# Gate and value as seven block products of 256 columns in place of two accumulations of 512, in an attention and gated feed-forward kernel

## The chip, the cores and the metric

The kernel runs on one core of a Trainium2 chip. The metric is the device time of one execution in microseconds (us). The kernel before took 1326.7 us, the median of three runs (1326.5 to 1326.91).

## The reference

```python
def phi(x):                                   # q is 8 x 8 x 576 x 64, w_phi 64 x 128
    proj = np.einsum('bhsd,df->bhsf', x, w_phi)
    proj = proj - np.max(np.abs(proj), axis=-1, keepdims=True)
    return np.concatenate([np.exp(proj), np.exp(-proj)], axis=-1)
q_p, k_p = (phi(q), phi(k))
kv = np.einsum('bhsf,bhsd->bhfd', k_p, v)
num = np.einsum('bhsf,bhfd->bhsd', q_p, kv)
den = np.einsum('bhsf,bhf->bhs', q_p, np.sum(k_p, axis=2))[..., None] + 1e-06
x = (num / den), heads side by side: 4608 tokens x 512
rms = np.sqrt(np.mean(x * x, axis=-1, keepdims=True) + 1e-06)
xn = x / rms * rms_g
g = xn @ w_gate                               # 512 x 1536
silu = g * (1.0 / (1.0 + np.exp(-g)))
val = xn @ w_val                              # 512 x 1536
out = silu * val @ w_out                      # 1536 x 512
```

## The kernel before

Every matrix is kept as a high part and a remainder in the type fp32r (`_split`: the high part by ScalarE, L60, and the remainder, the "low", by VectorE (DVE) or GpSimd (POOL), L61). A product is three matmuls: high weight by high x, high weight by low x, low weight by high x.

The work goes in three stages. The attention stage writes x transposed to DRAM (`xs`) and decodes the feed-forward weights, which arrive as 8-byte numbers (`_decode`, L48 to L55: two ScalarE passes, DVE passes L50, L51, L52, two GpSimd products L54, a DVE addition L55). Within it and just behind it, gate and value of the first `J1` = 3 column tiles are computed from x not yet normalised ("fills", L461) and stored as `gvs`.

The gate/value stage is the place of the change. It takes the tokens in nine blocks of `T` = 512 and the remaining `JN` = 9 column tiles of 128. For each block and tile `gv` (L641) accumulates gate and value in one PSUM bank each, in 2 x 12 matmuls of 128x512. The banks come from a pool of six, `gp`; two further banks, `fp`, serve the row sums. `hidden` applies silu to the gate bank on ScalarE (L626), multiplies by the value bank on DVE (L628) and stores h to DRAM. `gv_raw` (L652) brings the three tiles of the fills into the same path: it multiplies them by the reciprocal norm `ri` on DVE, then `hidden`.

While a block's tiles run, `prep(bk + 1)` prepares the next block in seven pieces, placed behind tiles 0, 2, 3, 4, 5, 6 and 7: load x; squares on ScalarE added up on GpSimd (L571, L572); a sum over partitions by two matmuls with ones (L580, L581) and a square root on ScalarE (L583); reciprocals (L587) and the normalised x (L592) on DVE; the split of x into `xb` with its lows on GpSimd. The pieces of `decs` decode w_out, 24 of them, one behind every second tile; `load_o` forms the sums of w_out that the output stage uses (L671). A Tile framework adds the waits; each engine executes its instructions in the order in which the code issues them.

```python
for n, j in enumerate(order):
    gv(bk, j)
    if n % 3 == 1:
        gv_raw(bk, n // 3, r.pop(n // 3))
    ...
    if n in pieces:
        pieces[n]()
    if (bk, n) in slots:
        slots[bk, n]()
```

The output stage (matmul line L802) multiplies h by w_out in 18 groups of 256 tokens. It uses seven products of block sums already, 126 matmuls of 128x256 a group.

## Time and profile before

| | |
|---|---|
| median of three runs | 1326.7 us |
| the profiled execution, its time and its span | 1327.53 us, 1325.0 us |
| TensorE (PE) busy, whole span | 1286.6 us (97%) |
| DVE, ScalarE (ACT), GpSimd (POOL) busy | 901.7, 689.9 and 645.3 us |
| mean granted TensorE clock | 0.993 |
| attention stage, with most fills | 0 to 505 us |
| last fills | 505 to 592 us |
| gate/value stage | 592 to 1049 us |
| output stage | 1049 to 1322 us |

In the lines of the profile, a group is "line engine operation, output<-inputs, shape and type, count | busy us, mean ns of one | idle time of the engine just before it and what ended it". A line of the timeline begins with the start and the duration in us; matmul durations there overlap, so the pace is read from the starts. A line of windows gives the window, its length, the busy time of each engine with the number of instructions, the granted clock in parts of full speed, the share of the DMA engines' time and GB/s. PEld is TensorE's loading of weights, which runs beside its matmuls.

### The profile page before, as it was taken

Reading aid. Unit: us, or ns where it says so; the run is one execution under the profiler, and the core shown is the slowest. Engines: PE = TensorE matmul, PEld = TensorE weight load, DVE = VectorE, ACT = ScalarE, POOL = GpSimd, SP = SyncE. Lnnn points to the kernel's source line nnn. Section 1 sums busy time; section 2 is a strip of 40 time slices with the busy share of each in tenths; the row PEclk is TensorE's granted clock in tenths of the full one; section 3 lists DMA queues with packets and bytes.
Section 4 is the critical chain, followed back from the end, with each engine's and each line's share of the span. In section 5 each row is a group of like instructions: output and inputs, shape, how many; then the busy total and the mean of one; then the engine's idle time right before and its main releaser. Section 6 shows DMA issues by size and latency. Waiting matters only on the chain. (4 is left out here: it accounts for less than half of the span.)

```text
span 1325.0 us, 23881 instructions
## 1 busy us (share of the span) xinstructions
PE 1286.6 (97%) x8742; PEld 1188.3 (90%) x8742; DVE 901.7 (68%) x1232; ACT 689.9 (52%) x1455; POOL 645.3 (49%) x580
## 2 busy tenths in 40 slices
PE   7989999999999989999999999999999999999998
PEld 7989999999999989998888877888888799999998
DVE  7898888788878763214366663665344389989994
ACT  5987877788777774453244333333232243433431
POOL 3765655556555563631141322421310178888884
PEclk9999999999999999999999999999999999999999
DMA  5556666665556529633343535544326134543441
GB/s 157 130 143 159 162 175 173 181 179 160 158 174 171 151 64 267 225 127 98 132 164 127 182 115 176 176 139 147 127 95 206 57 112 128 168 151 128 156 163 48
DMA packets 195299, 197.10 MB, mean 149 GB/s; under 512 B 68784, under 2 KB 151856, under 8 KB 195184
## 3 DMA queue, kind: packets, MB, share of 16 engines
q1 hardware_dynamic: 195184, 195.60, 48.6%
q8 instruction: 69, 1.13, 0.4%
q14 instruction: 46, 0.38, 0.1%
HBM read 126.04 MB, written 69.50 MB: 148 GB/s over the span
## 5 line engine op out<-in xcount | busy, mean ns | idle before, releaser
L641 PE MATMUL gp<-xb,w 128*128 128x512 f32 x1296 | 302.5, 393 | 1.7 <-DVE h L628 1.7
L641 PEld LDWEIGHTS gp<-xb,w 128*128 128x128 f32 x1296 | 243.4, 188 | 58.0 <-DVE h L628 3.0
L367 POOL TENSOR_TENSOR ql<-eq,qh 128x256 fp32r<-128x256 f32 x256 | 217.2, 879 | 76.2 <-issue 52.6
L61 POOL TENSOR_TENSOR xo<-st,xo 128x768 fp32r<-128x768 f32 x54 | 124.2, 2312 | 112.2 <-ACT xo L60 112.2
L54 POOL TENSOR_TENSOR wa<-raw,wa 128x192 f32<-128x192 f32 (+1 forms) x112 | 64.9, 600 | 165.8 <-DVE wa L52 120.0
L302 DVE TENSOR_REDUCE mx<-pp 128x4 f32<-128x512 f32 (+1 forms) x160 | 101.1, 633 | 47.7 <-PE pp L300 46.0
L338 PE MATMUL acc<-vm,ek 128*128 128x65 f32 x1024 | 131.4, 268 | 0.6 <-ACT ek L325 0.5
L338 PEld LDWEIGHTS acc<-vm,ek 128*128 128x128 f32 x1024 | 127.3, 192 | 1.2 <-ACT ek L325 1.2
L60 ACT CAST xo<-st 128x768 fp32r<-128x768 f32 x54 | 43.4, 835 | 152.0 <-DVE st L755 75.0
L626 ACT ACTIVATE sl<-gp 128x512 f32<-128x512 f32 x81 | 48.0, 594 | 135.4 <-PE gp L641 115.3
L61 POOL TENSOR_TENSOR xb<-x,xb 128x1024 fp32r<-128x1024 f32 x18 | 50.7, 2834 | 139.1 <-ACT xb L60 139.1
L628 DVE TENSOR_TENSOR h<-sl,gp 128x512 f32<-128x512 f32 x81 | 55.2, 683 | 87.9 <-PE gp L641 56.6
L363 ACT ACTIVATE qh<-sm 128x512 fp32r<-128x512 f32 (+1 forms) x192 | 97.2, 506 | 0.0
L461 PE MATMUL fp<-xo,fg 128*128 128x288 f32 x576 | 93.2, 301 | 2.7 <-ACT fo L464 2.2
L298 PE MATMUL pp<-wh,th 128*128 128x256 f32 x288 | 87.8, 306 | 2.7 <-DVE yr L305 2.1
L362 ACT ACTIVATE eq<-sm 128x512 f32<-128x512 f32 x128 | 78.4, 613 | 18.2 <-PE sm L351 17.4
L652 DVE TENSOR_TENSOR gvr<-gvr,ri 128x1024 f32<-128x1024 f32 x27 | 33.1, 1228 | 78.1 <-DMA gvr<-gvs 77.9
L461 PEld LDWEIGHTS fp<-xo,fg 128*128 128x128 f32 x576 | 81.1, 190 | 4.1 <-ACT fo L464 3.3
L300 PE MATMUL pp<-wh,tl 128*128 128x256 f32 x288 | 83.1, 297 | 1.3 <-DVE tl L61 1.3
L802 PE MATMUL gy<-wh,xo 128*128 128x256 f32 x432 | 80.1, 283 | 2.4 <-ACT xo L60 1.4
L299 PE MATMUL pp<-wl,th 128*128 128x256 f32 x288 | 81.7, 285 | 0.0
L641 PE MATMUL gp<-xb,fv 128*128 128x512 f32 x324 | 79.8, 395 | 1.0 <-DVE h L628 1.0
(167 smaller groups left out, 3428.5 us busy)
## 6 DMA issues: line engine op xcount, KB each, us to landing
hs<-h SPq DMA_DIRECT2D x108, 256.0 KB
gvs<-fo SPq DMA_DIRECT2D x96, 144.0 KB
gvr<-gvs SPq DMA_DIRECT2D x27, 512.0 KB
fg<-hs SPq DMA_DIRECT2D x9, 1536.0 KB
fv<-hs SPq DMA_DIRECT2D x9, 1536.0 KB
rc<-di SPq DMA_DIRECT2D x32, 288.0 KB
x<-xs SPq DMA_DIRECT2D x16, 576.0 KB
x<-xs SPq DMA_DIRECT2D x9, 1024.0 KB
```

The source lines that it names most:

```text
L61: (lo_eng or nc.vector).tensor_tensor(lo, x, hi.bitcast(F32), ALU.subtract)
L298: nc.tensor.matmul(o, th[:, cs], wh, start=True, stop=False)
L299: nc.tensor.matmul(o, th[:, cs], wl, start=False, stop=False)
L300: nc.tensor.matmul(o, tl[:, cs], wh, start=False, stop=True)
L302: nc.vector.tensor_reduce(mx[:, 0:2 * m], pp[:, 0:2 * m], axis=AX.X, op=ALU.max, apply_absolute_value=True)
L338: nc.tensor.matmul(acc[:, sg, h], e[h][:, sg, j], vm[:, h, j], start=False, stop=(h == 1 and j == T0 - 1))
L362: nc.scalar.activation(ei[:, sg], yi, AF.Exp, scale=1.0 - 2.0 * sg)
L363: nc.scalar.activation(hi[:, sg], yi, AF.Exp, scale=1.0 - 2.0 * sg)
L367: nc.gpsimd.tensor_tensor(lo[:, sg, cs], ei[:, sg, cs], hi[:, sg, cs].bitcast(F32), ALU.subtract)
L461: nc.tensor.matmul(fp[:, 0:TF], w, xx[x][:, c], start=(i == 0), stop=(i == 3 * NC - 1))
L641: nc.tensor.matmul(o, w, e[:, c], start=(i == 0), stop=(i == 3 * NC - 1))
L802: nc.tensor.matmul(place[n], a[:, kp], w[:, o], start=(first and kp == 0 and i == 0), stop=(kp == KP - 1 and i == 2), skip_group_check=True)
```

## The change

The two 512-wide accumulations become one 2 x 2 block product by the Strassen-Winograd scheme: the rows of the left matrix are gate and value, those of the right one the halves `LO` and `HI` (256 tokens each) of the block, and the inner dimension is halved too. A unit (block and tile) is then seven products p1 to p7, each 6 matmuls of 128x256 over 256 of the 512 inner values.

- *Accumulators.* Three banks, `A`, `B` and `E`, with two buffers each, in place of the six `gp`. p1 and then p2 go to A (the gate of LO). ScalarE copies p1's sum from A into B, where p6 is added; ScalarE copies that to SBUF as `u2`, then p7 is added; DVE adds B to `c22` (ScalarE's copy of p5 from E), then p4 is added to B: the value of LO. p3 is added to E, and DVE adds E to u2: the gate of HI. c22 is the value of HI. silu follows on ScalarE, the product for LO on DVE (L719), that for HI on GpSimd (L723).
- *Order.* `product` fixes the order on TensorE with `issue_after`; the old unit's p7, p3 and p4 stand between products of the new one: p1, p5, p7 of the old, p2, p6, p3 and p4 of the old.
- *Operands.* `prep` makes seven splits 512 wide for each block (four block sums on DVE, lows on GpSimd) in place of two 1024 wide, and `prep_w` the seven sums of the weights once, for six tiles during the last fills and for three in block 0.
- *Elsewhere.* `gv_raw` goes in halves of 256 tokens: product with `ri` on DVE (L737), silu on ScalarE, product on GpSimd (L739). The jobs are placed by a table `jobs` at four points of a unit. All of w_out's sums are formed in the last block, into slots of gate/value weights that are done with; decodes run in blocks 1 to 6, four each. The fills use two `fp` and two `A` banks in place of two `fp` and six `gp`; `raws` has two buffers in place of three; the h of the output stage goes to three slots in place of two.

```diff
-    ps_g = pool(pg_ctx, "m_ps_g", 6, space=PSUM)
-    gp = lambda: ps_g.tile([128, 512], F32, name="gp")
+    ps_g = pool(pg_ctx, "m_ps_g", 2, space=PSUM)
+    bank = lambda n: ps_g.tile([128, 512], F32, name=n)
...
+    def product(o, n, x, w, first):
+        last = next(i for i in reversed(nc.cur_bb.bb.instructions) if i.engine == mybir.EngineType.PE)
+        with tc.issue_after(last):
+            product_(o, n, x, w, first)
+
+    def product_(o, n, x, w, first):
+        i = 0
+        for c in range(2):
+            wh, wl = (w[:, h, ROW[n], c] for h in range(2))
+            xh, xl = (x[n][:, h, c] for h in range(2))
+            for a, e in ((wh, xh), (wh, xl), (wl, xh)):
+                nc.tensor.matmul(o, a, e, start=(first and i == 0), stop=(i == 5), skip_group_check=True)
+                i += 1
...
+            if n == 1:
+                u.A = bank("A")[:, LO]
+                product(u.A, 1, u.x, u.w, True)
+                u.B = bank("B")[:, LO]
+                nc.scalar.copy(u.B, u.A)
+            elif n == 5:
+                u.E = bank("E")[:, LO]
+                product(u.E, 5, u.x, u.w, True)
+                u.c22 = wk.tile([128, HT], F32, name="c22", bufs=3)
+                nc.scalar.copy(u.c22, u.E)
+            elif n == 2:
+                product(u.A, 2, u.x, u.w, False)
+                u.h = wk.tile([128, T], F32, name="h", bufs=3)
+                nc.scalar.activation(u.h[:, LO], u.A, AF.Silu)
+            elif n == 6:
+                product(u.B, 6, u.x, u.w, False)
+                u.u2 = wk.tile([128, HT], F32, name="u2")
+                nc.scalar.copy(u.u2, u.B)
+            elif n == 7:
+                product(u.B, 7, u.x, u.w, False)
+                nc.vector.tensor_tensor(u.c22, u.B, u.c22, ALU.add)
+            elif n == 3:
+                product(u.E, 3, u.x, u.w, False)
+                nc.vector.tensor_tensor(u.u2, u.E, u.u2, ALU.add)
+            elif n == 4:
+                product(u.B, 4, u.x, u.w, False)
+                nc.vector.tensor_tensor(u.h[:, LO], u.h[:, LO], u.B, ALU.mult)
+
+        def end(u):
+            nc.scalar.activation(u.u2, u.u2, AF.Silu)
+            nc.gpsimd.tensor_tensor(u.h[:, HI], u.u2, u.c22, ALU.mult)
+            nc.sync.dma_start(out=hsv[:, J1 + u.j, u.bk * T:(u.bk + 1) * T], in_=u.h)
...
+        u = Unit(bk, j)
+        u.p(1)
+        if older:
+            older.end()
+        hook(0)
+        u.p(5)
+        if old:
+            old.p(7)
+        hook(1)
+        u.p(2)
+        u.p(6)
+        hook(2)
+        if old:
+            old.p(3)
+            old.p(4)
+        hook(3)
+        older, old = old, u
```

TensorE in the second block, where the row sums for the next block fall. The rows give the line, the output, the two inputs, the shape and what a row waits for (names end in a buffer number, the waits name an engine's semaphore). Before, the fourth tile, the sums and the gate of the fifth:

```order
L641 MATMUL gp_9352<-xb_9100,w3_7934 128x512 [waits Activation_49]
L641 MATMUL gp_9352<-xb_9100,w3_7934 128x512 x11
L641 MATMUL gp_9365<-xb_9100,w3_7934 128x512 [waits DVE_49]
L641 MATMUL gp_9365<-xb_9100,w3_7934 128x512 x11
L580 MATMUL fp_9383<-sq_9335,ones_84 128x512
L581 MATMUL fp_9383<-sl_9336,ones_84 128x512 [waits Pool_49]
L641 MATMUL gp_9388<-xb_9100,w4_7936 128x512 [waits Activation_49]
L641 MATMUL gp_9388<-xb_9100,w4_7936 128x512 x11
```

After, one unit, with the first row sum of the next block's preparation inside it:

```order
L680 MATMUL A_9738<-xo_9334,w3_8169 128x256 x6
L680 MATMUL E_9759<-xo_9370,w3_8169 128x256 [waits DVE_49]
L680 MATMUL E_9759<-xo_9370,w3_8169 128x256 x5
L680 MATMUL B_9668<-xo_9572,w2_8091 128x256 [waits Activation_49]
L680 MATMUL B_9668<-xo_9572,w2_8091 128x256 x5
L609 MATMUL fp_9833<-t_9811,ones_87 128x512 [waits Activation_49]
L680 MATMUL A_9738<-xo_9491,w3_8169 128x256 [waits Activation_49]
L680 MATMUL A_9738<-xo_9491,w3_8169 128x256 x5
L680 MATMUL B_9745<-xo_9521,w3_8169 128x256 [waits DVE_49]
L680 MATMUL B_9745<-xo_9521,w3_8169 128x256 x5
L680 MATMUL E_9679<-xo_9589,w2_8091 128x256 x6
```

A tile is now seven short runs over three banks, two of them of the tile before (w2), and four of the runs wait for ScalarE or DVE.

ScalarE in the same block: the square root of the preparation and what stands around it. Before:

```order
L626 ACTIVATE sl_9378<-gp_9352 128x512 [waits DVE_49,PE_49]
L583 ACT_TABLE_LOAD
L583 ACTIVATE ri_9386<-fp_9383,eps_66 128x512 [waits PE_49]
L626 ACT_TABLE_LOAD [waits DVE_49]
L626 ACTIVATE sl_9414<-gp_9388 128x512 [waits PE_49]
```

After:

```order
L710 COPY u2_9792<-B_9745 128x256 [waits PE_49,Pool_49]
L611 ACT_TABLE_LOAD
L611 ACTIVATE ri_9736<-fp_9833,eps_66 128x512 [waits PE_49]
L722 ACT_TABLE_LOAD
L722 ACTIVATE u2_9709<-u2_9709 128x256 [waits DVE_49]
L697 COPY B_9822<-A_9815 128x256 [waits DVE_49,PE_49]
L702 COPY c22_9844<-E_9837 128x256 [waits PE_49]
```

The copy from A to B, L697, which the next unit's products on B need, now stands behind the square root and both table loads, and itself waits for DVE.

DVE in the same place. Before:

```order
L587 RECIPROCAL ri_9386<-ri_9386 128x256 [waits Activation_49]
L587 RECIPROCAL ri_9386<-ri_9386 128x256
L671 TENSOR_TENSOR wt_11434<-wc_11316 128x256 [waits DMAHW6_49,DMAHW5_49]
L50 TENSOR_SCALAR wp_9429<-wa_9430 128x256 [waits Activation_49]
L592 SCALAR_TENSOR_TENSOR x_9237<-x_9237,g_68,ri_9386 128x512 [waits DVE_49]
L592 SCALAR_TENSOR_TENSOR x_9237<-x_9237,g_68,ri_9386 128x512 x3
L51 SCALAR_TENSOR_TENSOR wp_9429<-wa_9430,wp_9429 128x256 [waits DVE_49]
L628 TENSOR_TENSOR h_9416<-sl_9414,gp_9401 128x512 [waits DMAHW2_49,PE_49]
```

After (reciprocals L615 ahead of these rows, normalisation L619):

```order
L713 TENSOR_TENSOR c22_9766<-B_9745,c22_9766 128x256 [waits PE_49]
L737 TENSOR_TENSOR gvr_10114<-gvr_10114,ri_9736 128x512 [waits DMAHW5_49,DMAHW1_49,DVE_49]
L737 TENSOR_TENSOR gvr_10266<-gvr_10266,ri_9736 128x512 [waits DMAHW1_49]
L619 SCALAR_TENSOR_TENSOR x_9613<-x_9613,g_68,ri_9736 128x512 [waits DMAHW5_49,DVE_49]
L619 SCALAR_TENSOR_TENSOR x_9613<-x_9613,g_68,ri_9736 128x512
L716 TENSOR_TENSOR u2_9792<-E_9759,u2_9792 128x256 [waits PE_49]
L50 TENSOR_SCALAR wc_9711<-wc_9711 128x256 [waits DMAHW6_49,Activation_49]
L619 SCALAR_TENSOR_TENSOR x_9613<-x_9613,g_68,ri_9736 128x512 x2
L737 TENSOR_TENSOR gvr_10181<-gvr_10181,ri_9736 128x512
L719 TENSOR_TENSOR h_9784<-h_9784,B_9745 128x256 [waits DMAHW1_49,PE_49]
```

Before, four normalisations and the reciprocals stood ahead of one product h. After, a product h (L719) has the reciprocals, four normalisations and three gvr products ahead of it, and the u2 addition (L716), which frees an E bank, stands in their midst.

More of the change, by code (lines that the diff above doesn't have):

```diff
@@ new lines, with prep_w, one_, two @@
+    W = {}
+    ROW = {1: 0, 2: 1, 4: 2, 3: 3, 6: 4, 5: 5, 7: 6}
+    def prep_w(j, pl):
+        d = {}
+        def one_():
+            d["w"] = w = raws.pop(j)
+            W[j] = pl.tile([128, 2, 7, 2, 128], F32R, name=f"w{j}")
+            d["sub"], d["p"] = sums7(w, W[j])
+            d["sub"](4, 0, 3)
+            d["sub"](3, 3, 2, ALU.add)
+            d["p"][0]()
+            d["p"][1]()
+        def two():
+            d["sub"](2, 3, 0)
+            d["sub"](1, 1, 2)
+            d["p"][2]()
+            d["p"][3]()
+        return [one_, two]
@@ L603, with split @@
-    pre = prep(0)
-    ahead = [pre[0], lambda: split_gv(0), lambda: raw_gv(3), lambda: split_gv(1), pre[1], lambda: raw_gv(4), pre[2],
-             lambda: split_gv(2), lambda: raw_gv(5)] + pre[3:] + [lambda j=j: split_gv(j) for j in range(3, JL)]
+            nc.vector.scalar_tensor_tensor(x[:, c], x[:, c], g[:, c:c + 1], ops["ri"], ALU.mult, ALU.mult)
+        part = lambda k, h: d["x"][:, 2 * k:2 * k + 2, h * HT:(h + 1) * HT]
+        def split(n, v, lo):
+            o = xp.tile([128, 2, 2, HT], F32R, name="xo")
+            _split(nc, o[:, 0], o[:, 1], v, lo_eng=lo)
+            ops[n] = o
@@ L606 @@
+    first, rest = prep(0)
+    ahead = []
+    for j in range(JL):
+        ahead += prep_w(j, wl6) + [lambda j=j: raw_gv(j + 2)]
+    pre = first + rest
+    ahead = [ahead[0], pre[0]] + [p for ab in zip(ahead[1:], pre[1:]) for p in ab] + pre[len(ahead):]
     n = 0
+    at_once = -(-len(ahead) // RES)
     while units or here or fills:
         if len(units) <= 6 and here:
-            units.extend(fill(*here.pop(0), nc.gpsimd, [fp, gp]))
+            units.extend(fill(*here.pop(0), nc.gpsimd, [fp, lambda: bank("A")]))
@@ L610 @@
         units.pop(0)()
-        if ahead and n % 2:
-            ahead.pop(0)()
-        n += 1
+        for _ in range(at_once):
+            if ahead:
+                ahead.pop(0)()
         load_x()
@@ L646, in load_r @@
-    def load_r(bk, j):
-        r = wk.tile([128, 2, T], F32, name="gvr", bufs=2)
-        nc.sync.dma_start(out=r, in_=gvv[j][:, :, bk * T:(bk + 1) * T])
-        return r
-    def gv_raw(bk, j, r):
-        nc.vector.tensor_tensor(r, r, xb[bk][1].unsqueeze(1).broadcast_to([128, 2, T]), ALU.mult)
-        hidden(bk, j, r[:, 0], r[:, 1])
-    W11, W21, W22, WT1, WT2, WT3, WT4 = range(7)
+    pad(ctx, RPAD, side="right")
+    wr3 = pool(ctx, "w_r", 1, side="right")
+    k_ctx = ExitStack()
+    wk = pool(k_ctx, "wk", 2, side="right")
@@ L688, in hload @@
     def hload(gi):
[L689 removed]
+        j = LAST[HSLOT[gi % 3]]
+        h = (wl6 if j < JL else wr3).tile([128, NJ, 256], F32, name=f"w{j}")
         nc.sync.dma_start(out=h, in_=hsv[:, :, gi * 256:(gi + 1) * 256])
         hts[gi] = h
[L693 to L698 removed]
@@ L699 @@
[L699 to L726 removed]
+    jobs = {}
@@ L727 @@
+    older.end()
+    for n in (7, 3, 4):
+        old.p(n)
+    old.end()
+    for key in sorted(jobs):
+        for p in jobs.pop(key):
+            p()
+    hload(1)
+    wos_ops = [wos_ops[kp] for kp in range(KP)]
+    k_ctx.close()
     g_ctx.close()
     pg_ctx.close()
+    pad(ctx, OPAD)
     xop = ctx.enter_context(tc.tile_pool(name="oop", bufs=16, reuse_waits="tile"))
-    ow = ctx.enter_context(tc.tile_pool(name="ow", bufs=2, reuse_waits="tile"))
+    ost = ctx.enter_context(tc.tile_pool(name="ost", bufs=2, reuse_waits="tile"))
```

293 lines of the change are left out of this document (161 added, 132 removed).

## The prediction

> **What bounds the kernel now.** I read the busy time by stage first (windows cut where the gate/value matmuls begin and end), then TensorE's pace inside the stages, its chain of waits, and then the groups of instructions.
>
> ```profile
> core 0: us, PE busy (x) PEld busy (x) DVE busy (x) ACT busy (x) POOL busy (x), PEclk, DMA share, GB/s
> 505.00:592.00 87.00, 82.95 (x616) 81.38 (x616) 18.98 (x23) 42.18 (x91) 39.70 (x26) 1.00 0.68 215
> 592.00:1049.00 457.00, 454.28 (x1961) 368.19 (x1960) 232.22 (x313) 153.53 (x247) 102.33 (x92) 1.00 0.43 141
> 1049.00:1065.00 16.00, 13.47 (x92) 12.38 (x91) 12.58 (x9) 6.55 (x9) 9.26 (x5) 0.89 0.05 17
> 1065.00:1322.00 257.00, 254.00 (x2180) 252.81 (x2178) 228.77 (x173) 94.45 (x134) 204.32 (x86) 1.00 0.41 134
> ...
> 640.00:690.00 50.00, 50.00 (x218) 1.00 0.43 143
> 1120.00:1160.00 40.00, 40.00 (x356) 1.00 0.46 145
> ...
> PE gp L641 <- DVE h L628: 2.7, 4, 1.1
> ```
>
> The change lives in the second window, 592 to 1049. TensorE is busy 454 of 457 us there at full clock; DVE has half, ScalarE a third, GpSimd a fifth. In all 457 us TensorE waits 2.7 us for another engine, so the stage is bound by TensorE's matmuls alone, and the last wait to end is never another engine's. The two pace rows (PE alone) give 50/218 = 0.229 us for a 128x512 matmul in this stage and 40/356 = 0.112, say 0.113 us, for a 128x256 one, taken from the output stage, which runs such matmuls already.
>
> What is less plain is why the block's preparation, which runs beside, does no harm. These rows are from the timeline of one block's preparation of the next, then the source line of the product with silu:
>
> ```profile
> 720.47 3.36 DVE L587 RECIPROCAL ri<-ri 128x256 f32<-128x256 f32 x2
> 723.89 2.07 DVE L592 SCALAR_TENSOR_TENSOR x<-x,g,ri 128x512 f32<-128x512 f32 x3
> 726.46 5.58 POOL L61 TENSOR_TENSOR xb<-x,xb 128x1024 fp32r<-128x1024 f32 x2 [6.96 <-ACT xb L60]
> 726.87 0.68 DVE L628 TENSOR_TENSOR h<-sl,gp 128x512 f32<-128x512 f32 x1
> 727.47 2.31 DVE L628 TENSOR_TENSOR h<-sl,gvr 128x512 f32<-128x512 f32 x1
> 729.70 2.49 DVE L52 TENSOR_SCALAR wa<-wp 128x256 int32<-128x256 int32 x1
> ...
> L628 DVE TENSOR_TENSOR h<-sl,gp x81: 673/681/690, 597.8 to 1049.5; 128x512 f32<-128x512 f32 x81
> L628 DVE TENSOR_TENSOR h<-sl,gvr x27: 679/693/2308, 603.9 to 1044.6; 128x512 f32<-128x512 f32 x27
> ```
>
> GpSimd's two subtractions run from 726.46 to 732.04, each 2.8 us. A DVE product with one input in PSUM takes 0.68 us among them, and none of 81 took more than 0.69. The same product with both inputs in SBUF took 2.31 us, and the decode's copy 2.49 instead of 0.29: both end where one of GpSimd's ends. So a DVE instruction of this kind stands still until GpSimd's running one is over, and everything behind it in DVE's queue with it. Here DVE is full from 720.5 to 732, and TensorE lost almost nothing, because six accumulation banks lie between it and DVE's product.
>
> **The change part by part.** *Matmuls.* Per unit (a block and a column tile) 24 of 128x512 become 7 x 6 = 42 of 128x256: 81 x 42 x 0.113 = 384.4 us, and 18 row sums of 128x512 add 4.1. Against 457: a gain of 68.5 us. A product takes 0.68 us, a unit 4.75.
>
> *Banks and order.* The other stages keep their matmuls. But the accumulators now are A, B and E with two buffers each, and a unit passes through other engines between its products: ScalarE copies A to B after p1 (one must have a free B), E to c22, then silu; copies B to u2 before p7; DVE adds B to c22 before p4 may write B. The order on TensorE is fixed, so one late instruction stops all behind it. Rows for what these cost:
>
> ```profile
> L583 ACT ACT_TABLE_LOAD x9 | 11.5, 1283 | 0.2
> L583 ACT ACTIVATE ri<-fp,eps 128x512 f32<-128x512 f32 x9 | 6.2, 689 | 8.2 <-PE fp L581 8.2
> L807 ACT COPY os<-fp 128x256 f32<-128x256 f32 x18 | 6.5, 363 | 4.5 <-PE fp L802 4.5
> ...
> L652 DVE TENSOR_TENSOR gvr<-gvr,ri 128x1024 f32<-128x1024 f32 x25 | 30.7, 1229 | 78.1 <-DMA gvr<-gvs 77.9
> L587 DVE RECIPROCAL ri<-ri 128x256 f32<-128x256 f32 x16 | 26.9, 1722 | 1.3 <-ACT ri L583 1.3
> L592 DVE SCALAR_TENSOR_TENSOR x<-x,g,ri 128x512 f32<-128x512 f32 x32 | 22.1, 745 | 0.2
> L52 DVE TENSOR_SCALAR wa<-wp 128x256 int32<-128x256 int32 x24 | 15.8, 660 | 0.7
> L55 DVE TENSOR_TENSOR wa<-wp,wa 128x256 f32<-128x256 f32 x24 | 13.4, 557 | 29.2 <-POOL wa L54 29.2
> L61 DVE TENSOR_TENSOR wl<-wt,wh 128x1024 fp32r<-128x1024 f32 x6 | 8.4, 1404 | 0.0
> L821 DVE TENSOR_TENSOR ro<-gz,uu 128x256 f32<-128x256 f32 x18 | 7.6, 424 | 0.6
> L50 DVE TENSOR_SCALAR wp<-wa 128x256 int32<-128x256 int32 x24 | 7.0, 292 | 1.8 <-ACT wa L48 1.8
> L671 DVE TENSOR_TENSOR wt<-wc,wt 128x256 f32<-128x256 f32 x12 | 5.0, 420 | 0.1
> ...
> L61 POOL TENSOR_TENSOR xo<-st,xo 128x768 fp32r<-128x768 f32 x54 | 124.2, 2312 | 112.2 <-ACT xo L60 112.2
> L572 POOL TENSOR_TENSOR ss<-ss,sq 128x512 f32<-128x512 f32 x27 | 35.2, 1303 | 71.5 <-ACT sq L571 71.5
> L54 POOL TENSOR_TENSOR wa<-raw,wa 128x128 f32<-128x128 f32 x48 | 22.3, 487 | 105.4 <-DVE wa L52 92.3 <-issue 11.2 <-POOL xb L61 1.9
> 386.60 0.74 POOL L369 TENSOR_TENSOR ql<-eqr,qh 128x256 fp32r<-128x256 f32 x1
> ```
>
> A unit free of preparation has five ScalarE passes of 0.36 and three DVE passes of 0.42, under half of 4.75: covered. Its copies lie a product or more ahead of their readers, so no wait there.
>
> *One block boundary, walked.* I set 0 at p1 of the fourth unit of a block; with both row sums the unit ends at 5.2. ScalarE's u2 copy ends at 4.2; table load 1.28, square root 0.69, table load again: 7.45; then the held silu and the bank copy, 8.2. p2 of unit 5, due at 7.3, starts at 8.3: 1.0 lost. DVE's reciprocals end at 6.25 + 3.44 = 9.7, c22's addition at 10.1. Ahead of h of unit 4 now stand three gvr products (half of 1229 and a little: 0.69), four normalisations (0.745), u2 (0.42) and L50 (0.29): h at 16.2 if nothing holds DVE. But GpSimd meanwhile multiplies h HI and gvr (0.72 to 0.74 each) and takes the lows of the first operand (512 wide, 1.3 by the sums' row), about 3.5 us of which DVE's two-SBUF work must sit out: 19.7. Unit 6 shares B with unit 4; its bank copy, and so p2, comes at 20.3 instead of 13.1: 7.2 lost (3.6 without holds). Behind h stand L51, the third, c22, two more gvr, L52, a subtraction, u2, L55, a subtraction, h of unit 5: at 28.0 (22.4 without), p2 of unit 7 loses 3.5 (1.3). Per boundary **11.7 with holds, 5.9 without**. I take 11.7, since the rows at 726 show DVE held in the same work; GpSimd's steps are shorter now but more. All this work is in the kernel before too; its cover (six banks) is what goes.
>
> *Sum.* Six boundaries 70.2. The last one has no decode steps ahead (0.29 + 0.42 + 0.29 + 0.42 on DVE, 2 x 0.49 on GpSimd): 9.3. Block 0, which also forms the sums of three weight tiles (lows 1.40 on DVE, 2.3 on GpSimd, each three times): 11, between 9 (no decodes, lows hidden) and 17 (half of the lows on the path). The last block forms W_out's sums: 24 x 0.42 + 6 x 1.40 on DVE and 6 x 2.3 on GpSimd, 32 us that exclude one another, with the units' and gvr's 15 about 47 in 43: 3 taken, 0 to 6. It takes as much off the blocks before. Hand-over to the output stage: a silu before its first cast, 1 (0 to 3). Fills: weight sums beside 42 of 87 busy us on ScalarE and 19 on DVE, four banks instead of eight: 0 (0 to 4), hidden by matmuls that are 95% of that window. Nothing for the smaller loads: the DMA share is 0.43. Total lost 94.5, gained 68.5: +26 on the profiled execution's 1327.5, or **1353** by the median 1326.7, 0.8 below it.
>
> One price is disputed. After the square root's table load the next instruction started 0.02 us later:
>
> ```profile
> 819.79 1.28 ACT L583 ACT_TABLE_LOAD   x1
> 821.09 0.69 ACT L583 ACTIVATE ri<-fp,eps 128x512 f32<-128x512 f32 x1
> ```
>
> The Trainium skill, "ScalarE: Activation LUTs", section "What ACT_TABLE_LOAD costs", adds a drain of about 1380 ns to each 1283 ns load. By it the reciprocals would start 1.4 us later at seven boundaries, an estimated 10 us more (1363); this row shows no drain, so the measurement decides and the sum has none.
>
> **The rivals.** *B, the holds miss DVE.* If GpSimd's work falls beside the reciprocals and PSUM readers, a boundary costs 5.9. Then 35.4 + 4.5 + 9 + 3 + 1 = 53: 15 us faster, 1311. It decides in this direction once a boundary costs under 7.9, since (68.5 - 15)/6.8 = 7.9 (15 for start, end and hand-over; the last boundary counted as 0.8). For it: of 27 gvr products the median is 0.693, unheld. Against: after halves the work that shares the time.
>
> *C, all but the table loads is hidden* (1.0 at each boundary, 12 in all): 1270. Against: it needs DVE to run h ahead of the normalisations, which its order does not.
>
> *D, it cancels* within 0.2% (2.7 us, about what a measurement can tell from no change): 1324 to 1329.
>
> *E, the stops also cost clock.* At the hand-over TensorE nearly stood still from 1054.9 to 1057.6:
>
> ```profile
> 1054.43 0.39 PE L802 MATMUL gy<-wh,xo 128*128 128x256 f32 x2
> 1054.77 0.28 PE L802 MATMUL gy<-wh,xo 128*128 128x256 f32 x1
> 1057.61 0.50 PE L802 MATMUL gy<-wh,xo 128*128 128x256 f32 x2 [0.66 <-POOL xo L61]
> 1058.47 0.41 PE L802 MATMUL gy<-wl,xo 128*128 128x256 f32 x1
> 1058.68 0.63 PE L802 MATMUL gy<-wh,xo 128*128 128x256 f32 x2
> ```
>
> Then a matmul took 0.41 and two 0.63 in place of 0.28 and 0.39, so each stands 0.21 behind the one before instead of 0.113, and this lasted some 3.5 us: 1.75 lost. In a boundary the slow stretch after the second stop ends in the third and is free; after the third it costs 1.75, times seven 12: 1366, up to 1378 if both cost. For it: stops of 7.2 and 3.5 us are longer than this one. Against: in the walk a product or two runs inside them. The Trainium skill, "TensorE: Matmul & The Clock Gate", section "Why this matters for your kernels", allows no idle gap over about 3 us between bursts, which by it makes E the likely one wherever the walk holds.
>
> **How the numbers follow.** The forecast 0.52 (1335 to 1360: boundaries of 9.5 to 12.5); B 0.24 (1300 to 1324); E 0.14 (1360 to 1378); C 0.05; D 0.05. Faster 0.29, same 0.05, slower 0.66. Forecast and B share the one unknown, DVE's holds, so the range takes in both and most of E: 1300 to 1375, leaving out C and the tails; the forecast's own is 1335 to 1360.
>
> **What would show it.** The stage 592 to 1049 as about 483 us, with TensorE busy some 80%; the matmuls at 0.113 inside a unit without preparation. TensorE's chain of waits led by A/B's matmuls waiting for ScalarE's bank copy and E's for DVE's u2, in eight clusters, with DVE's gvr products and normalisations above 0.69 and 0.745 on the mean. For B: these means as before and the stage near 440. For E: granted clock below 1 in windows of a boundary. I am wrong altogether if DVE's h comes ahead of the normalisations, or if a unit without preparation takes more than 4.8 us.

## The result, and the profile after

The changed kernel takes 1374.0 us (median of four runs, 1371.3 to 1383.9) against 1326.6 for the kernel before on the same chip: 1.037 times as long, 95% interval 1.032 to 1.042. The forecast was 1353, so the direction was right; the time lies 21 us above it, 14 above the forecast's own bounds (1335 to 1360) and 1 us inside the wide range (1300 to 1375). The profiled execution took 1373.07 us, its span is 1371.3; the 46.3 us between this span and the 1325.0 of before are what is explained here.

The windows of the changed kernel's last fills and of its gate/value stage (the columns are named in the first row):

```profile
core 0: us, PE busy (x) PEld busy (x) DVE busy (x) ACT busy (x) POOL busy (x), PEclk, DMA share, GB/s
505.00:560.00 55.00, 41.10 (x262) 39.21 (x262) 35.91 (x33) 28.25 (x51) 33.85 (x21) 0.84 0.55 167
560.00:610.50 50.50, 46.41 (x335) 45.94 (x334) 13.13 (x11) 20.00 (x46) 24.36 (x17) 0.97 0.46 154
610.50:1097.70 487.20, 425.94 (x3421) 414.12 (x3419) 324.78 (x513) 269.41 (x641) 278.40 (x276) 0.96 0.40 134
```

The last fills end at 610.7 where they ended at 592.0: 18.7 us lost before the stage that the change is about has begun. The stage itself takes 487 us for 457: 29.8 lost. The output stage with its hand-over, 1097.5 to 1371.3, is 2.2 shorter than before (273.8 for 276.0), though its first matmuls stand 5.4 us for ScalarE (the row of gy below). 18.7 + 29.8 - 2.2 = 46.3.

TensorE's waits, whole span (who waits, for whom; us in total, times, longest):

```profile
PE A L680 <- ACT B L697: 36.4, 25, 3.3
PE E L680 <- DVE u L716: 18.8, 14, 3.3
PE A L467 <- ACT fo L470: 9.2, 1, 9.2
PE fp L467 <- ACT fo L470: 6.6, 3, 2.8
PE gy L959 <- ACT xo L60: 5.6, 2, 5.4
PE B L680 <- DVE c L713: 3.9, 4, 1.7
```

Before, TensorE waited 2.7 us for DVE in this stage. Now it waits 55 us for ScalarE's copy from A to B and for DVE's sum that frees E, the two that the prediction named, and 3.9 for DVE's addition to c22. Two rows of the fills (L467) have grown to 15.8 us from 2.2.

**The stage by blocks.** The starts of its 3402 matmuls, taken in groups of 42, give each block's length. At 0.113 a block is 42.7 us, or 43.2 with its row sums; worked out so, the nine blocks took

```
block      0     1     2     3     4     5     6     7     8
us       60.2  51.8  52.1  52.1  58.7  52.0  58.0  52.1  49.9   (486.9)
over     17.0   8.6   8.9   8.9  15.5   8.8  14.8   8.9   7.2   (98.6)
```

A group without preparation takes 4.76 us (42 x 0.1133), as forecast, and in some stretches 4.95. A boundary (blocks 1, 2, 3, 5, 7) loses 8.8. It looks like this on all engines (timeline of the changed kernel, block 2 of the table: start, us, engine, line, [idle before <- what ended it]; rows put in order of time):

```profile
739.49 0.37 ACT L710 COPY u<-B 128x256 f32<-128x256 f32 x1 [0.35 <-POOL wc L54]
739.88 1.28 ACT L611 ACT_TABLE_LOAD   x1
743.50 0.37 ACT L697 COPY B<-A 128x256 f32<-128x256 f32 x1
743.92 0.98 PE L680 MATMUL A<-xo,w 128*128 128x256 f32 x6 [0.79 <-ACT B L697]
745.46 1.28 DVE L737 TENSOR_TENSOR gvr<-gvr,ri 128x512 f32<-128x512 f32 x2
746.66 1.88 DVE L619 SCALAR_TENSOR_TENSOR x<-x,g,ri 128x512 f32<-128x512 f32 x2
748.46 0.41 DVE L716 TENSOR_TENSOR u<-E,u 128x256 f32<-128x256 f32 x1
748.93 0.97 PE L680 MATMUL E<-xo,w 128*128 128x256 f32 x6 [1.20 <-DVE u L716]
749.20 2.42 DVE L619 SCALAR_TENSOR_TENSOR x<-x,g,ri 128x512 f32<-128x512 f32 x2
749.27 1.81 POOL L61 TENSOR_TENSOR xo<-x,xo 128x512 fp32r<-128x512 f32 x1
751.55 1.20 DVE L737 TENSOR_TENSOR gvr<-gvr,ri 128x512 f32<-128x512 f32 x1
752.68 0.41 DVE L719 TENSOR_TENSOR h<-h,B 128x256 f32<-128x256 f32 x1
753.53 1.24 PE L680 MATMUL A<-xo,w 128*128 128x256 f32 x6 [2.92 <-ACT B L697]
754.56 1.48 PE L680 MATMUL B<-xo,w 128*128 128x256 f32 x6
757.98 0.73 PE L680 MATMUL A<-xo,w 128*128 128x256 f32 x5
```

Read it from the end. The matmuls at 753.53 waited 2.92 us for ScalarE's copy into a B bank. That bank came free with DVE's h at 752.68. h was late because DVE did three gvr products and four normalisations first, and of these the two at 749.20 took 1.21 each in place of 0.7: GpSimd's subtraction ran from 749.27 to 751.08 beside them. Then six matmuls took 1.48 in place of 0.87: the granted clock was 0.50 until 757.5, and the first product at full pace again is the one at 757.98.

The same hold in the groups of the stage (mean ns behind the busy us); without holds the prediction reckoned with 690 and 745:

```profile
L737 DVE TENSOR_TENSOR gvr<-gvr,ri 128x512 f32<-128x512 f32 x54 | 48.2, 910 | 4.1 <-DMA gvr<-gvs 3.7 <-issue 0.3
L619 DVE SCALAR_TENSOR_TENSOR x<-x,g,ri 128x512 f32<-128x512 f32 x32 | 34.9, 1131 | 0.0
```

Blocks 4 and 6 lose 6 to 7 us more than the others, each to a late load. In block 4 ScalarE stood 3.96 us for the load of x, with the copy into B behind it in its queue (first three rows). In block 6 it was another load: DVE stood 3.25 us, and later 2.23, for raw tiles of W_out at the head of its queue, with the sum that frees E behind them (last row). The code issues these sums of W_out in block 8:

```profile
837.89 0.63 ACT L591 ACTIVATE ri<-x 128x512 f32<-128x512 f32 x1 [3.96 <-DMA x<-xs]
839.77 0.36 ACT L697 COPY B<-A 128x256 f32<-128x256 f32 x1
840.19 1.65 PE L680 MATMUL A<-xo,w 128*128 128x256 f32 x6 [3.31 <-ACT B L697]
984.44 0.42 DVE L544 TENSOR_TENSOR wc<-wc 128x256 f32<-128x256 f32 x1 [3.25 <-DMA wc<-wos]
```

**The fills.** The timeline of the changed kernel around the longest stop:

```profile
517.33 1.05 ACT L549 CAST w<-wc 128x1024 fp32r<-128x1024 f32 x1 [2.66 <-DVE wc L544]
525.85 0.63 ACT L591 ACTIVATE ri<-x 128x512 f32<-128x512 f32 x1 [7.48 <-DMA x<-xs]
527.43 0.38 ACT L470 COPY fo<-fp 128x288 f32<-128x288 f32 x1
528.16 3.25 PE L467 MATMUL A<-xo,fv 128*128 128x288 f32 x12 [9.18 <-ACT fo L470]
```

A cast of a weight sum (L549) and the squares of block 0 (L591) stand in ScalarE's queue ahead of the copies that empty the fills' banks (L470); the cast waits 2.7 us for DVE, then the first square 7.5 for x. So ScalarE begins no such copy between 514.3 and 527.4. TensorE fills the four banks it has and stands 9.2 us; then it runs at half clock (12 matmuls in 3.25 us, 1.76 at full clock).

One thing in the description ahead has to be put right: the engines do not execute in the order in which the code issues. The scheduler moves ScalarE's and DVE's instructions; the rows of the order shown there (three gvr products ahead of h) are its choice, and the squares above and block 6's sums of W_out were moved forward in the same way.

### The profile page after: what moved, and what is told of

Same layout as the page of the kernel before. It is cut to its first block, busy times and chain, and to the rows that moved or that the text cites. A ratio compares the mean times of both kernels' runs of the same rounds, so it can differ in the third digit from the quotient of the medians.

```text
span 1371.3 us, 28126 instructions
## 1 busy us (share of the span) xinstructions
PE 1258.1 (92%) x10202; PEld 1233.9 (90%) x10202; DVE 1023.6 (75%) x1451; ACT 809.1 (59%) x1849; POOL 843.2 (61%) x775
## 3 DMA queue, kind: packets, MB, share of 16 engines
q1 hardware_dynamic: 206560, 195.60, 46.5%
## 5 line engine op out<-in xcount | busy, mean ns | idle before, releaser
L680 PE MATMUL B<-xo,w 128*128 128x256 f32 x1458 | 215.1, 285 | 5.7 <-DVE c L713 3.9
L680 PEld LDWEIGHTS B<-xo,w 128*128 128x128 f32 x1458 | 193.4, 196 | 7.2 <-DVE c L713 4.9
L680 PE MATMUL A<-xo,w 128*128 128x256 f32 x972 | 147.2, 289 | 36.7 <-ACT B L697 36.4
L680 PEld LDWEIGHTS A<-xo,w 128*128 128x128 f32 x972 | 129.4, 196 | 43.0 <-ACT B L697 42.3
L680 PE MATMUL E<-xo,w 128*128 128x256 f32 x972 | 144.0, 285 | 18.9 <-DVE u L716 18.8
L680 PEld LDWEIGHTS E<-xo,w 128*128 128x128 f32 x972 | 127.7, 194 | 22.8 <-DVE u L716 22.7
L723 POOL TENSOR_TENSOR h<-u,c 128x256 f32<-128x256 f32 x81 | 70.5, 870 | 96.8 <-ACT u L722 75.1
L61 POOL TENSOR_TENSOR xo<-x,xo 128x512 fp32r<-128x512 f32 (+1 forms) x72 | 106.3, 1488 | 26.1 <-ACT xo L60 25.0
L467 PE MATMUL fp<-xo,fg 128*128 128x288 f32 x576 | 97.3, 308 | 8.1 <-ACT fo L470 6.6
L467 PEld LDWEIGHTS fp<-xo,fg 128*128 128x128 f32 x576 | 84.7, 196 | 9.8 <-ACT fo L470 7.7
L61 POOL TENSOR_TENSOR xo<-w,xo 128x768 fp32r<-128x768 f32 x36 | 91.6, 2543 | 0.0
L959 PE MATMUL gy<-w,xo 128*128 128x256 f32 x648 | 79.5, 281 | 6.2 <-ACT xo L60 5.6
L959 PEld LDWEIGHTS gy<-w,xo 128*128 128x128 f32 x648 | 76.9, 192 | 7.1 <-ACT xo L60 6.0
```

Of the source, the lines that this page charges most:

```text
L61: (lo_eng or nc.vector).tensor_tensor(lo, x, hi.bitcast(F32), ALU.subtract)
L467: nc.tensor.matmul(fp[:, 0:TF], w, xx[x][:, c], start=(i == 0), stop=(i == 3 * NC - 1))
L680: nc.tensor.matmul(o, a, e, start=(first and i == 0), stop=(i == 5), skip_group_check=True)
L723: nc.gpsimd.tensor_tensor(u.h[:, HI], u.u2, u.c22, ALU.mult)
L959: nc.tensor.matmul(place[n], a[:, kp], w[:, o], start=(first and kp == 0 and i == 0), stop=(kp == KP - 1 and i == 2), skip_group_check=True)
```

## The experiments

Ratios are to the kernel before, with 95% intervals; block lengths are found as above. Kernels with the fills as in the change (the change, e2, e5, e7) begin the gate/value stage at 609.6 to 612.7 in their profiled executions, one each; that is the spread against which a start is to be read. e3 and e6 leave the fills alone but alter block 0's preparation, which runs beside them, and begin at 608.2 and 606.0.

**e1 to e4: are late squares the cause, or DVE's order?**

```diff
+    def behind(engine):
+        return tc.issue_after(next(i for i in reversed(nc.cur_bb.bb.instructions) if i.engine == engine))
...
+            with behind(mybir.EngineType.Activation):      # e1: block 0 alone; e2: blocks 1 to 8
+                square(c)
-    ahead = [ahead[0], pre[0]] + ...     # e1: the squares 2 to 4 fills later
+    ahead = ahead[:2] + [pre[0]] + ahead[2:14] + ...
-                job(bk, NS + (0 if n == 0 else 6 + n), ...)
+                job(bk, NS + (0 if n == 0 else 10 + n), ...)      # e2
+            with behind(mybir.EngineType.DVE):             # e3: gvr products, normalisations, sums
```

> The changed kernel, but the squares of block 0 stand some four fills further behind the load of x on ScalarE; banks, weight sums and everything else as in the change. Theory 1 (the squares wait for the load of x at the head of ScalarE's queue, the copies that free the fills' four banks stand behind them, and TensorE's clock falls in the stop): the gate/value stage begins near 595 instead of 610.7 and the whole takes about 1358 us. Rival (the fills lose 18 us to four banks in place of eight and to the weight sums on DVE, wherever the squares stand): the stage begins at 607 to 611, the whole stays at 1370 to 1374.

1378.7, ratio 1.040 (1.037 to 1.043); the stage begins at 612.4. The squares wait 1.5 us for x in place of 10.0, but the next late piece takes their place at the head of ScalarE's queue, a cast of a weight tile whose load has not landed (timeline of e1):

```profile
529.15 0.83 ACT L547 CAST w<-wc 128x768 fp32r<-128x768 f32 x1 [9.74 <-DMA wc<-wvs]
```

> The changed kernel, but in blocks 1 to 8 the squares of the next block come one unit later behind the load of x; the fills as in the change. Theory 1: the blocks that took 58 us (the fifth and the seventh) come down to the 52 of the others, about 12 us less, 1361 us. Rival (these two blocks lose to something else, such as the stores of h or the decode): they stay at 58, 1373 us. Under both the 8.7 us that every block loses around its fifth and sixth unit stay.

1410.2, 1.064 (1.060 to 1.068). Blocks 57 long, worse by 5, with groups of 10.5 to 13.9 us: it seems that preparation that begins a unit later crowds what follows it. Blocks 4 and 6 keep 2.5 and 4.5 us of their excess; in block 6 the late load is not x.

> The changed kernel, with DVE's order fixed where the preparation meets the units: gvr products, normalisations and block sums stand behind the last DVE instruction written before them, so that the units' additions and h come between them. Theory 2 (what stands ahead of h and u2 on DVE sets the 8.7 us of a boundary): the loss falls to 3 to 5 us a block, 35 us over eight blocks, about 1338 us. Rival (GpSimd's holds and the half clock set it, whatever the order): the loss stays at 7 us or more, 1360 us or above.

1365.0, 1.030 (1.024 to 1.036). h comes in time: TensorE's waits for the copy into B fall from 36.4 to 4.1 us. Yet blocks 1 to 6 take 53 to 58 us. The long group of a boundary still takes 9.3 to 9.4, since the reciprocals, whose place is not fixed here, now stand ahead of the addition to c22 (first row, TensorE's waits); and a part of the loss has moved to the first group of a block (7.6 to 8.8 us), where the decode's steps now meet the splits' lows (timeline of e3, DVE's copy and GpSimd's subtractions). The gain comes from blocks 0 and 7, 49.8 and 48.9 in place of 60.2 and 52.1.

```profile
PE B L686 <- DVE c L719: 20.3, 11, 2.8
715.78 2.74 POOL L61 TENSOR_TENSOR xo<-x,xo 128x512 fp32r<-128x512 f32 x2
717.43 1.23 DVE L52 TENSOR_SCALAR wc<-wc 128x256 int32<-128x256 int32 x1
719.05 0.97 PE L686 MATMUL E<-xo,w 128*128 128x256 f32 x6 [1.98 <-DVE u L722]
```

L52 took 0.29 where nothing ran beside it.

> The three edits together: squares behind the load in the fills and in the blocks, and DVE's order fixed. If the three causes are apart from one another, the gains add: 15 + 12 + 35 us from 1373, about 1311 us, below the kernel before. If one stop only hides another, 1330 us or more.

1385.1, 1.045 (1.041 to 1.050). The waits for the copy into B are gone here too (4.0 us), but TensorE stands 21.9 us, eight times, for the operand of the row sums: the later squares are what comes late now.

**e5 and e6: the holds.**

```diff
-            nc.scalar.activation(u.u2, u.u2, AF.Silu)                       # e5
-            nc.gpsimd.tensor_tensor(u.h[:, HI], u.u2, u.c22, ALU.mult)
+            nc.scalar.activation(u.h[:, HI], u.u2, AF.Silu)
+            nc.gpsimd.tensor_tensor(u.h[:, HT:HT + 16], ..., u.c22[:, 0:16], ALU.mult)
...                                                                         # the gvr product (L739) likewise
-        P, V = nc.gpsimd, nc.vector                                         # e6: the splits' lows
+        P, V = nc.vector, nc.vector
```

> The changed kernel with most of two GpSimd products left out: silu times value for the upper half of a block (L723) and the gvr product (L739) are formed in 16 of 256 columns only, so GpSimd has some 11 us less to do in a block; nothing else is left out. Holds theory (DVE instructions with two SBUF inputs stand still while GpSimd works): gvr products, normalisations and block sums come down from 0.91, 1.13 and 1.27 us on the mean to nearly 0.7, and a boundary loses about 6 us instead of 8.7, near the 5.9 that the prediction had without holds; about 1350 us. Rival (only the length of DVE's queue counts): 8.7 stays, 1370 us.

1361.3, 1.027 (1.025 to 1.030). The means of DVE's held instructions fall: gvr products from 910 to 746 ns, normalisations from 1131 to 969, block sums (L633) from 1271 to 1096. Blocks 1, 3, 5 and 7 last 49.6 to 51.1, so some 7.0 are lost in place of 8.8 (block 2, with a further stop of 2.25 us in its second group, lasts 53.4). The group with the longest stop falls from 9.61 to 8.43, the one behind it from 6.86 to 4.9 in the later blocks.

> The changed kernel with the lows of the seven operands of a block on DVE in place of GpSimd: DVE has 7 x 0.69 = 4.8 us more in a block, GpSimd 9 to 10 us less, and what the two exclude one another from is some 4 us less. Holds theory: a boundary loses less than 8.7, 6 to 7 us, 1355 to 1360 us. Rival (length of DVE's queue): it loses 10 us or more, 1385 us.

1353.2, 1.022 (1.020 to 1.024). The lows, some 10 us a block on GpSimd, now lie on DVE, which has more to do already, and yet the boundaries become shorter, 50.4 to 51.5, and the late loads in blocks 4 and 6 cost less (52.1 and 53.9). The same means are 788, 982 and 906 ns. Of the 20 us won on the spans, 4.7 lie ahead of the stage. e5 and e6 agree with the Trainium skill, "SBUF — State Buffer", section "SBUF: two separate sides": a GpSimd instruction that reads SBUF and a DVE instruction with two SBUF inputs exclude each other for the whole instruction. It names, beside these, DVE instructions in a two-port mode; L52 in e3, with one SBUF input, was held, and no run shows its mode.

**e7: the half clock.**

```diff
+                if u.j == 5 and u.bk < NB - 1:      # ahead of p2
+                    for _ in range(24):
+                        nc.tensor.matmul(spare[:, LO], ..., start=True, stop=True)
```

> The changed kernel with 24 matmuls of 128x256 into a spare bank, which nothing reads, ahead of p2 of each sixth unit, where TensorE stands still for 2.9 us before it runs at half clock: they fill 2.7 us of that stop. If the half clock costs time (rival E of the prediction): the slow matmuls behind the stop go away and every boundary is 2 to 2.5 us shorter, some 18 us in all, 1355 us. If the slow stretch only takes the place of a third stop, as the walk has it: at most 0.6 us a boundary, 1368 us or more, and a stop on DVE's h appears in the seventh unit.

1391.7, 1.050 (1.044 to 1.056). The timeline of e7, TensorE alone:

```profile
752.82 2.88 PE L709 MATMUL fp<-xo,w 128*128 128x256 f32 x24
756.78 0.87 PE L680 MATMUL B<-xo,w 128*128 128x256 f32 x6
762.41 1.65 PE L680 MATMUL E<-xo,w 128*128 128x256 f32 x6 [2.64 <-DVE u L722]
```

The stop is filled, and what follows runs at full clock (0.87 for six). Then TensorE comes to the next late instruction sooner and stands there for 2.64. But blocks 1, 2, 3 and 5 are 2 to 3 us longer than in the change, about what the 24 matmuls take, and the dummy products shifted DVE's order a little; so e7 alone doesn't price the half clock. The change itself does. Its block 5 has almost the same stops as block 2 (0.86, 1.32 and 2.94 us) and its clock stays at 1.00 behind them; yet it is as long, 52.0 for 52.1, because two further stops, 0.35 and 1.15, take the place of the slow stretch (timeline of the changed kernel, block 5):

```profile
916.35 0.96 PE L680 MATMUL A<-xo,w 128*128 128x256 f32 x6 [2.94 <-ACT B L697]
923.22 0.97 PE L680 MATMUL A<-xo,w 128*128 128x256 f32 x6 [1.15 <-ACT B L697]
```

So in a boundary the half clock costs little of its own: TensorE would wait for another engine in that time.

**e8, e9, e13, e15, e17 and e18: the fills, one suspected cause at a time.**

```diff
-            units.extend(fill(..., [fp, lambda: bank("A")]))
+            units.extend(fill(..., [lambda: next(turn)()] * 2))    # e8: fp, A, E; e18: fp, A, E, B
-        for _ in range(at_once):                                   # two pieces a fill
+        for _ in range(1 + n % 2):                                 # e9
-    at_once = -(-len(ahead) // RES)
+    at_once = 1                                                    # e15
-        ahead += prep_w(j, wl6) + [lambda j=j: raw_gv(j + 2)]
+        ahead += prep_w(j, wl6) + [lambda j=j: raws.update({j + 2: kept[j % 2]}) ...]    # e13, with e1's squares
+            if 0 < j < JL:                                         # e17, in prep_w
+                W[j] = W[0]
+                return
```

> The changed kernel, but the last fills use six banks in turn (fp, A and E, two each) instead of four. If the missing banks are the reason why a late piece on ScalarE stops TensorE in the fills: each of the two long stops is about 3.2 us (two fills) shorter, the stage begins at 602 to 605 instead of 610.7, 1365 us. If the queue of ScalarE alone sets it: no change, 1373 us.

1368.8, 1.034 (1.032 to 1.035); the stage begins at 604.1, 5.5 ahead of the spread.

> The changed kernel, but the pieces of preparation beside the last fills are handed out at 1.5 a fill on the mean instead of 2 (before the change it was one for two fills). If loads that are not there yet at the head of ScalarE's queue cost the fills their time: each piece has a third more time, the stops shrink and the stage begins at 600 to 606 instead of 610.7, 1365 us. If it is the amount of work on ScalarE and DVE: no change, 1373 us.

1370.6, 1.030 (1.027 to 1.032); 607.8, hardly outside the spread.

> The changed kernel with the squares of block 0 some six fills later, and without the loads of four raw gate/value tiles beside the fills (the tiles before them are used again: that data is left out, all work on it stays). If ScalarE's waits for x and for raw tiles at the head of its queue make the loss in the fills: the long stops there go away with four banks and all casts and sums in place, and the stage begins at 594 to 598 instead of 610.7, 1358 us. If the amount of work on ScalarE and DVE makes it: the stage begins at 605 or later.

1368.8, 1.034 (1.029 to 1.039); 608.3 and not 594 to 598. Without late loads the stops fall on DVE's sums of the weights, and on the row sums, which TensorE itself executes in its order (timeline of e13):

```profile
546.46 1.04 ACT L549 CAST w<-wc 128x1024 fp32r<-128x1024 f32 x1 [5.62 <-DVE wc L544]
548.08 1.22 PE L616 MATMUL B<-t,ones 128*128 128x512 f32 x2 [5.86 <-ACT t L60]
```

> The changed kernel, with one single edit: one piece of preparation beside each of the last fills instead of two (before the change it was one beside every second), so that the pieces are spread over some 42 fills and not 21. Banks, squares and all work stay. If ScalarE's queue is blocked because too many pieces, each waiting for a load, for DVE or for a sum, stand among the copies that free the fills' banks: the stage begins at 596 to 602 instead of 610.7, about 1362 us. If four banks alone make the loss: it begins at 607 or later, 1370 us.

1376.2, 1.040 (1.036 to 1.044); 613.8, no gain at all: the squares are still moved forward by the scheduler, and one wait for a fill's copy is 7.5 long.

> Only the fills' weight work changes: the sums and splits are formed for one of six weight tiles, which all six then use (left out: the sums of the other five; their loads stay). Four banks and two pieces per fill as in the change. Pieces theory (late weight pieces at the head of ScalarE's queue are what stops the fills): one stop, that of the squares waiting for x (7.5 us), is left at most, and the gate/value stage begins at 596 to 601. Cover theory (four banks do not carry ScalarE's ordinary copies over the sixteen squares, norms and splits of block 0 either): it begins at 606 or later.

1374.7, 1.035 (1.028 to 1.041); 605.5. Five sixths of the weight work are worth about 5 us. This falls between the two expectations, nearer to cover; a stop of 7.1 for a fill's copy is left.

> Only the banks change: the fills go round all eight (two each of fp, A, E and B), as many as before the change; two pieces per fill and the hoisted squares stay. Cover theory (the eight banks were what hid late pieces): the stage begins at 592 to 597, with no wait of TensorE for a fill's copy above 2 us. Pieces theory (a piece that waits 7 to 10 us for a load outlasts eight banks too, at 1.36 us a bank about 10 us from full to empty, and the pieces are four times as dense): 600 to 605, little better than six banks (604.1).

1379.6, 1.037 (1.032 to 1.043); 607.5. Waits for a fill's copy are gone from the list, as the cover theory had it, and yet only some 3 us are won, less than with six: the stop has moved to the row sums (waits of TensorE in e18). A fill, by the way, takes 1.60 us (12 matmuls starting at 523.79 and the next at 525.39 in e16), not the 1.36 of the expectation.

```profile
PE B L607 <- ACT t L60: 10.0, 1, 10.0
```

**e10, e11, e12, e14 and e16: towards a better version.** In e10 reciprocals, normalisations, sums and splits are fixed on DVE in the gaps behind c22 and h, the lows of the splits go to DVE, and the decode is moved away from them. e11 adds six banks and 1.5 pieces a fill; e12 keeps the six banks with two pieces a fill, brings the squares together, moves the decode forward and puts the last block's sums behind h; e14 adds to e12 1.5 pieces a fill and later squares of block 0. e16 moves the preparation half a unit back, and takes one piece a fill and the last block as in the change.

```diff
+            with behind(mybir.EngineType.DVE):   # reciprocal, normalisation, sums, split, gvr
-        P, V = nc.gpsimd, nc.vector
+        P, V = nc.vector, nc.vector
-            for n in range(17):
-                job(bk, NS + (0 if n == 0 else 6 + n), ...)
+            for n, at in enumerate([4, 11, 12, 13, 14, 15, 18, ...]):     # e10
+            for n, at in enumerate([4, 11, 11, 12, 12, 14, 18, ...]):     # e12, e14
+            for n, at in enumerate([4, 13, 13, 13, 14, 16, 20, ...]):     # e16
```

> The changed kernel, fills as in the change, but in blocks 0 to 7 the preparation's DVE work (reciprocals, normalisations, sums, gvr products, and the lows, on DVE here) is written one or two pieces at a time right behind c22's addition or right behind h of a unit, with DVE's order fixed there, and the decode between. If queue order and holds together make the 8.7 us of a boundary: it falls to 2 or 3 us, the stage from 487 to about 440, the whole to 1325 us. If the two shared engines simply have too much work for 43 us a block: 6 us or more remain, 1350 us.

1362.3, 1.024 (1.021 to 1.028). Nearly all stops of the boundary are gone but one: 11.5 to 13.2 us in the group where TensorE has to execute the row sums. Waits of TensorE in e10:

```profile
PE fp L618 <- ACT t L60: 23.7, 8, 3.6
```

The squares were spread so far that the sum comes late, eight times.

> The same with six banks in the last fills and 1.5 pieces a fill. If the loss in the fills and the loss at the boundaries are independent: 8 to 12 us less than the same kernel without it, 1315 us, below the kernel before.

1355.3, 1.018 (1.016 to 1.021); begins at 606.5, blocks as in e10.

> As the run with DVE's order fixed (units' additions first, lows on DVE) and six banks in the fills, but the four squares follow one another right behind the load of x (there they were spread over two units and TensorE stood 4 to 8 us in each block for the sum's operand, the one stop that was left), the decode stands earlier in a block, and in the last block W_out's sums stand behind h or c22 as well. If that stop was the last one and no shared engine is full: the blocks come down from 52 to 45 or 46 us, the stage to 415 us, the whole to about 1300 us, below the kernel before. If GpSimd and DVE have too much work for a block of 43 us, another stop of 4 us or more takes its place: 1340 us or more.

1337.4, 1.010 (1.005 to 1.015). Blocks 47.5 to 49.3, the last one 55.0 (49.9 in the change). The stage is 447.8 long, 39 shorter than in the change. It begins at 611.2, with six banks: TensorE waits there for a split of the fills' x (4.5) and again for a copy (5.4).

> The kernel of the first of these three with the squares of block 0 later as well and 1.5 pieces a fill on the mean: if loads at the head of ScalarE's queue make what the fills still lose, the stage begins some 5 us earlier than there; if not, within 2 us of it.

1331.3 (10 runs), 1.006 (1.003 to 1.009); begins at 604.1.

> The fixed order on DVE with the lows there and the preparation half a unit later than in the run with the sums' operand in time, so that the squares no longer wait for x; W_out's sums in the last block as in the change; in the fills six banks, one piece a fill and the squares of block 0 later. If what is left is such waits: blocks of 46 to 48 us, the last block 50, the stage from about 597 to 1030, the whole 1300 to 1312 us, below the kernel before. If GpSimd and DVE lack the time: blocks stay at 48.5 or more and the whole at 1320 us.

1321.2 (12 runs, 1314.0 to 1329.1), 0.998 (0.996 to 1.001): some 50 us better than the change, and not to be told from the kernel before. Its windows, then TensorE's waits:

```profile
505.00:599.70 94.70, 85.01 (x601) 83.10 (x600) 47.77 (x49) 45.66 (x93) 43.71 (x26) 0.95 0.58 184
599.70:1038.70 439.00, 410.28 (x3420) 399.25 (x3418) 334.54 (x569) 270.62 (x646) 205.42 (x223) 1.00 0.46 149
```

```profile
PE A L696 <- ACT B L713: 14.5, 21, 1.4
PE E L696 <- DVE u L732: 6.9, 17, 1.0
```

The stage is 18 us shorter than the 457 of before, the fills end 7.7 later, and the hand-over with the output stage takes 282.5 where it took 276.0: 6.5 more. 18.0 - 7.7 - 6.5 = 3.8, the difference of the spans (1325.0 and 1321.2). No stop in the stage is longer than some 1.5 us, the granted clock is 1.00, and a boundary loses 3.3 to 5 (blocks 1 to 5 and 7: 46.5 to 48.2).

## Why the prediction was right and wrong, step by step

*Matmuls.* Right: groups at 4.76 us, 68.5 us gained on paper. All of it was spent, and more.

*The stage.* Forecast 68.5 gained and 93.5 lost, so 482; measured 487.

| term | forecast | measured |
|---|---|---|
| six boundaries | 70.2 (35.4 without holds) | 65.5, of which some 12.6 are late loads, of x in block 4 and of W_out in block 6 |
| the last boundary | 9.3 | 8.9 |
| block 0 | 11 (9 to 17) | 17.0 |
| the last block | 3 (0 to 6) | 7.2 |
| hand-over and output stage | 1 (0 to 3) | -2.2 |
| fills | 0 (0 to 4) | 18.7 |

*The walk through a boundary* holds up to the first product h. With 0 at p1 of the fourth unit, which starts at 735.51: u2's copy ends at 4.4 (forecast 4.2), the bank copy at 8.4 (8.2) with 0.8 lost (1.0), and h at 17.6, between 16.2 without holds and 19.7 with all of them. The second stop came in two, 1.2 for E and 2.9 for A, 4.1 in place of 7.2. A third stop (3.5) did not come; in its place stands the half clock, which stretched 24 matmuls from 2.7 to 4.45. So 8.8 and not 11.7: of 3.5 us of holds that the walk put ahead of h about 1.4 fell there. The range between 5.9 and 11.7 held, and 52.9 from pure boundaries with 12.6 from late loads, which the walk didn't have, came near 70.2 by chance. That GpSimd's instructions hold DVE's is shown by e5 and e6; that DVE's order makes the long stop by e3, where the wait for the copy into B goes, and, with the lows moved too, by e10 and e16. The rest of the 8.8, some 2, is in block 2 a short fourth stop (0.2), matmul starts at each stop that lie some 0.3 further apart than its idle time, and 0.5 from 111 matmuls at the slower pace of the last section.

*Rival B* (53 us of loss) fell with the means of 910 and 1131. *Rival E*: its sign was there, a granted clock of 0.96 and 171 matmuls begun at half clock, which took some 16 us more than at full pace (the prediction reckoned 12). And 1374 lies in its bracket (1360 to 1378), but not by its mechanism: in block 5 later stops took the place of the slow stretch at no gain, as the prediction argued for the second stop, and without the fills' 18.7 the time would have been 1355. The busy share was 87% and not 80, in part because matmuls at half clock count as busy. The bound of 4.8 us for a unit without preparation was kept in most groups; 4.95 in others is not explained.

*Block 0 and the last block* were sized too low, by 6 and 4: within or a little over their ranges. In block 0 the order on DVE is most of it: with that order fixed, in e3, 6.6 are lost in place of 17.0. The last block loses 12 in e12 and e14, which have W_out's sums in other places, but 10 to 11 in e10 and e11, which have not, so what these places are worth stays open.

*The step that failed* is the fills: "0 (0 to 4), hidden by matmuls that are 95% of that window". 18.7 were lost: TensorE waited 15.8 us for the fills' copies (2.2 before), and its matmuls took 87.5 us for 83.0 at the lower clock (14.0 more idle and 4.6 more busy in the window). The error was to price the pieces by the busy time that they add. A busy TensorE is not cover: what hides a late piece is how long TensorE can go on with the banks it has, 1.60 us a fill and so 6.4 with four empty ones, while ScalarE began no copy out of a bank for 13.2 us, held by a sum and then by a load. No single cause carries the 18.7. Six banks give 5.5 to 6.6 back, five sixths of the weights' pieces about 5, the lows of block 0 on DVE 3.6 to 4.7 (e6), and eight banks, later squares, early loads or thinner pieces alone some 3 or less, since each time another late instruction stops the line: a cast (e1), a sum or a row sum (e13, e18). Six banks, one piece a fill and late squares, with the lows on DVE and its order fixed, together bring 11 (e16). How the other 7.7 divide stays open.

Had the fills been priced at 18.7, the sum would have given 1372.

## What to carry to other kernels

With an order fixed on one engine, cover is counted in banks times the time that fills one, against the longest time that the queue which empties them can be held, several waits in a row included; the busy share of the engine didn't show it here (95% of that window before, and 18.7 us lost). When such a stop is removed, look for the next late instruction before counting the gain: in e1, e3, e4, e10, e13 and e18 it took much or all of what was won. Taking 15% of a stage off TensorE paid only after the side engines' instructions had been put by hand where the fixed order has slack, and then it broke even (e16, 0.998) and no more.
